# One tile in two halves for the conversion of w_out, a later split of the second unit of factors, half as many unread products, masks loaded first

## The chip, the cores and the metric

The kernel runs on one core of a Trainium2 chip. The metric is the device time of one execution in microseconds (us). TensorE (PE) multiplies, VectorE (DVE) and ScalarE (ACT) work element by element, SyncE (SP) issues all DMAs of this kernel, and GpSimd (POOL) only fills a few constants. Each engine takes its instructions strictly in the order in which they were written for it; an instruction that waits for a semaphore holds up everything behind it on its engine.

## The reference

Inputs are float32 in the reference; the weights reach the chip as 64-bit patterns (float64), so the kernel has to turn them into float32 itself.

```python
# attention: 4 batches, 8 heads, 576 positions, 64 dims; heads 0-3 see a local window of 32,
# heads 4-7 see the positions at a stride of 32
scores = (q @ k.T) / 8 ; scores = where(mask, scores, -1e9)
attn   = softmax(scores) ; attn_out = attn @ v            # 2304 tokens x 512
# first gated block
a = x @ w1 ; b = x @ w2 ; h = (a * b) @ w3 ; x = h @ w_out # 512 -> 1024 -> 1024 -> 512
# second block
h = x @ w_in                                               # 512 -> 2048
g = h * (1 / (1 + exp(-1.702 * h)))
out = g @ w_out                                            # 2048 -> 512
```

## The kernel before

Every float32 matrix is held as a high and a low part in a rounded format; a product of two matrices is three matmuls (high by low, low by high, high by high). `split_hi` (L171, ACT) makes the high part, `split_lo` (L177, DVE) the low part.

A weight unit arrives as raw 64-bit words (1024 KB) and goes through `to_f32`: two ACT instructions (L192 writes the float32 tile, L193 rewrites half of the raw words in place), then three on DVE (L194, L195, L196).

Stage 1 is the attention of batch 0. ACT and DVE do the softmax and the first weight units; PE has little to do, and `busy` (L496 to L498) puts matmuls between whose result, in the tile `spare`, nothing reads: two for each of 44 places.

Then PE carries the rest: the first block of batches 0 to 3 (L354 makes the products with w1 and w2, L400 the product with the joined w3 and w_out, `ysb` L406 copies it out and `ydram` keeps it), with the attention of the next batch woven in. While batch 3 runs, the eight units of the second block's w_out (called here w_out units 1 to 8; 8 to 15 in the code) are converted by `u_conv` (L541): load the raw words (L538, tile `raw`, two of them, one in pool `cv_a`, one in `cv_b`), `to_f32` into the tile `x` (pool `cv_a`, one buffer), load the raw words of the unit after next, write `x` to DRAM (`wodram`, 512 KB, L555). The tile `x` has 2048 columns, of which w_out uses the first 1024.

The second block works on 768 tokens at a time with seven products per unit in place of eight (`quad`, L679 and on; eight units per 768 tokens). Its factors of w_in come from DRAM (`widram`) in `w_load` (L613), into the same tile `x`, and are split into `hl`. The units of w_out come back from `wodram` in `wt_load` (L641) through the `raw` tile of `cv_a`, and are split into `w`. A `quad` makes seven products of six matmuls each (L666); ACT copies the first one out of PSUM into a tile `c` (L684), DVE adds the others (L672), gelu (L657, L658), and `o_group` (L712) multiplies the gelu of the unit before by w_out, nine matmuls each, one group in the middle of the quad (`mid`) and one behind it. PSUM tiles `ps` come from the pool `mm` with four buffers: a fifth product waits until a copy has freed one.

The pool `p2`, from which `c` and the other small tiles of the second block come, is opened where the first block's pools and `cv_b` were closed, so its tiles lie where `ysb` and the `raw` tile of `cv_b` lay.

The order on each engine is made by a scheduler from the order of the program: `weave` sorts pieces of work by a place between 0 and 1, and the scheduler then moves an instruction ahead of others where its own estimate says that it is ready earlier. So edits at one place can change the order at another.

Of the kernel before, what the change touches and what calls it, by code (L numbers as in the profile page):

```python
# [11 lines left out]
F32 = mybir.dt.float32  # L12
F32R = mybir.dt.float32r
# [8 lines left out]
P = 128  # L22
# [22 lines left out]
CW2 = 1024  # L45
# [3 lines left out]
NB = NT // BT  # L49
NU = 8  # L50
# [87 lines left out]
def body(ctx: ExitStack, tc, qk, vv, mask, w1, w2, w3t, wo, win, wout, out):  # L138
    nc = tc.nc
# [29 lines left out]
    def split_hi(hi, src, eng="act"):  # L169
        if eng == "act":  # L170
            nc.scalar.activation(hi, src, AF.Copy)  # L171
        else:
            nc.vector.tensor_copy(hi, src)

    def split_lo(lo, src, hi, eng="dve"):
        e = nc.vector if eng == "dve" else nc.gpsimd
        e.tensor_tensor(lo, src, r(hi), op=ALU.subtract)  # L177
# [46 lines left out]
    def a_load(n):  # L224
        if n >= n_all or n in raws:
            return
        tl = ALL[n]
        nk, w = tl.nk, 2 * (tl.nq + tl.nk)
        t = at.tile([P, ATW], F32, tag="qk", name="qk", bufs=3)
        nc.sync.dma_start(t[:, :w], qk[n, :, :w])  # L230
        u = at.tile([P, HL * D], F32, tag="v", name="v", bufs=4)
        nc.sync.dma_start(u[:nk], vv[n, :nk])
        raws[n] = (t, u)
# [249 lines left out]

    nc.gpsimd.memset(band[0], 0.0)
    nc.gpsimd.memset(band[1], 0.0)
    a_load(0)
    nc.sync.dma_start(msk, mask)
    a_load(1)
    for i in range(2):
        c_load(i)  # L490
# [3 lines left out]
    nc.vector.tensor_copy(identb, ident)  # L494

    def busy():  # L496
        for _ in range(2):
            nc.tensor.matmul(spare, identb, msk.rearrange("p m n -> p (m n)"), start=True, stop=True)  # L498

    weave(steps_for(0), list(zip((0.1, 0.5), conv(0, 1))), [busy] * 44)  # L500
# [29 lines left out]
    cv = None  # L530
# [9 lines left out]

    def u_conv(i, last=False):  # L541
        raw = todo.pop(i)
        x = cv[0].tile([P, 2 * CW2], F32, tag="x", name="x")
        to_f32(x[:, :CW2], raw, CW2)
        if not last:
            u_load(i + 2)
        if i < NU:
            a21, a11, a12, a22, s1, s2, s3, s4 = (x[:, n * 256:(n + 1) * 256] for n in range(8))
            nc.vector.tensor_tensor(s1, a21, a22, op=ALU.add)
            nc.vector.tensor_tensor(s2, s1, a11, op=ALU.subtract)  # L550
            nc.vector.tensor_tensor(s3, a11, a21, op=ALU.subtract)
            nc.vector.tensor_tensor(s4, a12, s2, op=ALU.subtract)
            nc.sync.dma_start(widram[i], x[:, 256:])
        else:
            nc.sync.dma_start(wodram[i - NU], x[:, :CW2])  # L555

    def u_convs(lo, hi, ahead=True):
        return [lambda i=i: u_conv(i, not ahead and i + 2 >= hi) for i in range(lo, hi)]
# [51 lines left out]

    wq = {}

    def w_load(n):  # L613
        if n < NB * NU:
            t = (p2 if n % 2 else cv_a).tile([P, 2, 7 * 256], F32R, tag="hl", name="hl")
            x = cv_a.tile([P, 2 * CW2], F32, tag="x", name="x")[:, 256:]
            nc.sync.dma_start(x, widram[n % NU])
            split_hi(t[:, 0], x)
            split_lo(t[:, 1], x, t[:, 0])
            wq[n] = t  # L620

    g = batch_groups(3)
    weave(
        g, [(0.02 + 0.06 * kk, lambda kk=kk: y_prep(0, kk)) for kk in range(2)] + [(0.09, lambda: w_load(0))]
        + [(0.1, lambda: u_load(NU)), (0.11, lambda: u_load(NU + 1))]
        + [(0.14 + 0.7 * i / NU, f) for i, f in enumerate(u_convs(NU, 2 * NU))],
    )
    p1s.close()
    right2.close()
# [8 lines left out]
    gl, gr = {}, {}  # L638
    acc_l, acc_r = {}, {}

    def wt_load(i):  # L641
        t = cv_a.tile([P, CW2], I64, tag="raw", name="raw").bitcast(F32)[:, :CW2]
        nc.sync.dma_start(t, wodram[i])
        w = wt[i].rearrange("p a c n -> p a (c n)")
        split_hi(w[:, 0], t)
        split_lo(w[:, 1], t, w[:, 0])

    def g_split(src):
        t = ring[used[0] % len(ring)]
# [58 lines left out]
    def o_group(acc, g, i, half):  # L708

        for t in range(HT // P):  # L710
            for a, c in ORDER:
                nc.tensor.matmul(  # L712
                    acc[t], g[:, a, t * P:(t + 1) * P], wt[i][:, c, half],
                    start=(i == half == 0 and (a, c) == ORDER[0]),
                    stop=(i == NU - 1 and half == 1 and (a, c) == ORDER[-1]),
                )
# [8 lines left out]
                nc.scalar.activation(ob, acc[t], AF.Copy)  # L725
            nc.sync.dma_start(out[c0 + t * P:c0 + (t + 1) * P, :], ob)

    wt_load(0)
    w_load(1)
    for b in range(NB):  # L730
        left = [accp.tile([P, 512], F32, tag="acc", name="acc") for _ in range(HT // P)]
        for i in range(NU):
            if b == 0 and i + 1 < NU:
                wt_load(i + 1)
            quad(b, i, (lambda i=i: o_group(left, gl.pop(i - 1), i - 1, 0)) if i else (lambda: None))
            if i:
                o_group(left, gl.pop(NU + i - 1), i - 1, 1)
        for h in range(2):
            o_group(left, gl.pop(h * NU + NU - 1), NU - 1, h)
        put(left, b * BT)  # L740
        if b + 1 < NB:
            for kk in range(2):
                y_prep(b + 1, kk)
        right = [mm.tile([P, 512], F32, tag="mm", name="acc") for _ in range(HT // P)]
        for i in range(NU):
            for h in range(2):
                o_group(right, g_split(gr.pop(h * NU + i)), i, h)
        put(right, b * BT + HT)
# [35 lines left out]
```

## Time and profile before

| | us |
|---|---|
| median of 3 runs (lowest, highest) | 878.0 (876.34, 879.31) |
| the profiled execution's own time | 878.23 |
| its span, first to last instruction | 876.4 |
| PE busy in the span | 833.2 (95%) |
| DVE busy | 587.2 (67%) |
| ACT busy | 437.9 (50%) |
| mean granted clock of PE, 1 is 2.4 GHz | 0.982 |

Busy time is the union of an engine's instructions. Matmuls overlap one another, so the sum of their durations is more than the time they take. Times inside the trace count from the first instruction.

### The profile page before, as it was taken

How to read it: one execution, taken by the hardware profiler on the slowest of the kernel's cores; microseconds unless marked ns; L12 is line 12 of the kernel's file. 1: busy time of each engine (PE TensorE's matmuls, PEld its weight loads, DVE VectorE, ACT ScalarE, POOL GpSimd, SP SyncE). 2: the span in 40 equal slices, each digit the busy share in tenths (PEclk: the TensorE clock that was granted, in tenths of full speed). 3: DMA queues.
4: the chain of work that ended last, by engine and by line, in shares of the span. 5: the costliest groups of instructions: out<-in, count | busy, mean ns of one | idle time of the engine just before them, and what ended most of it. 6: DMA issues, size and time to landing. Idle time of an engine off the chain costs nothing.

```text
span 876.4 us, 14097 instructions
## 1 busy us (share of the span) xinstructions
PE 833.2 (95%) x5288; PEld 744.0 (85%) x5288; DVE 587.2 (67%) x1369; ACT 437.9 (50%) x996; POOL 1.4 (0%) x8
## 2 busy tenths in 40 slices
PE   6999999999999999999993399999999999999998
PEld 3589899987889999999993389988999988999986
DVE  5999882368767778656342688876487765677740
ACT  6998762257565464444332455554244543434430
POOL 0000000000000000000000000000000000000000
PEclk9999999999999999999997699999999999999999
DMA  7765551244577553133445445213222232222010
GB/s 258 245 218 174 167 188 58 68 145 156 200 248 231 190 189 117 56 141 127 138 148 164 162 141 188 86 43 109 82 95 73 81 106 87 79 84 85 1 37 36
DMA packets 41700, 114.03 MB, mean 130 GB/s; under 512 B 4512, under 2 KB 25888, under 8 KB 38048
## 3 DMA queue, kind: packets, MB, share of 16 engines
q1 hardware_dynamic: 41632, 113.13, 37.9%
q8 instruction: 41, 0.67, 0.3%
q14 instruction: 27, 0.22, 0.1%
HBM read 88.60 MB, written 24.51 MB: 129 GB/s over the span
## 4 chain that ended last, share of the span: by engine, by line
PE 75%; DMA 9%; DVE 7%; ACT 7%; issue 1%; SPq 0%; ACTq 0%; DVEq 0%
PE acc L712 22%; PE ps L666 19%; PE ps L354 18%; PE ps L400 8%; DMA wodram<-x 4%; PE acc L469 2%; PE sc L250 2%; PE pv L308 2%; ACT sm L260 2%; DMA raw<-in_wout 1%; DMA x<-widram 1%; PE spare L498 1%; DVE x L196 1%; DVE x L195 1%; PE pt L286 1%
## 5 line engine op out<-in xcount | busy, mean ns | idle before, releaser
L666 PE MATMUL ps<-yq,hl 128*128 128x384 f32 x1008 | 188.9, 342 | 27.6 <-ACT c L684 21.7
L666 PEld LDWEIGHTS ps<-yq,hl 128*128 128x128 f32 x1008 | 181.3, 191 | 32.9 <-ACT c L684 22.2
L712 PE MATMUL acc<-w,w 128*128 128x512 f32 x864 | 205.2, 391 | 1.2 <-ACT w L171 1.2
L712 PEld LDWEIGHTS acc<-w,w 128*128 128x128 f32 x864 | 161.3, 188 | 34.4 <-ACT w L171 2.2
L400 PE MATMUL ps<-ab,w 128*128 128x288 f32 x768 | 108.1, 298 | 1.3 <-DVE ab L177 1.3
L400 PEld LDWEIGHTS ps<-ab,w 128*128 128x128 f32 x768 | 102.5, 188 | 4.6 <-DVE ab L177 2.4
L354 PE MATMUL ps<-xbh,w 128*128 128x288 f32 x512 | 103.4, 295 | 0.0
L354 PE MATMUL ps<-xah,w 128*128 128x288 f32 x512 | 102.1, 295 | 0.0
L354 PEld LDWEIGHTS ps<-xbh,w 128*128 128x128 f32 x512 | 82.2, 188 | 0.1
L354 PEld LDWEIGHTS ps<-xah,w 128*128 128x128 f32 x512 | 81.9, 188 | 0.0
L354 PE MATMUL ps<-xbl,w 128*128 128x288 f32 x256 | 79.6, 311 | 0.0
L354 PE MATMUL ps<-xal,w 128*128 128x288 f32 x256 | 76.4, 299 | 0.9 <-ACT abf L377 0.8
L657 ACT ACTIVATE sg<-c 128x384 f32<-128x384 f32 x48 | 25.1, 525 | 103.7 <-DVE c L672 103.5
L260 ACT ACTIVATE sm<-sm,st 96x128 f32<-96x128 f32 (+2 forms) x176 | 67.7, 388 | 17.7 <-DVE st L255 17.6
L193 ACT ACTIVATE raw<-raw 128x1024 int32<-128x1024 uint32 (+1 forms) x44 | 42.7, 972 | 48.3 <-DMA raw<-in_wout 32.2
L672 DVE TENSOR_TENSOR u<-ps,u 128x384 f32<-128x384 f32 x96 | 53.2, 554 | 11.2 <-PE ps L666 9.1
L177 DVE TENSOR_TENSOR hl<-x,hl 128x1792 fp32r<-128x1792 f32 x24 | 48.6, 2024 | 16.4 <-ACT hl L171 16.4
L379 DVE TENSOR_TENSOR abf<-ps,abf 128x288 f32<-128x288 f32 x64 | 28.9, 451 | 37.8 <-PE ps L354 31.6
L354 PEld LDWEIGHTS ps<-xbl,w 128*128 128x128 f32 x256 | 48.0, 188 | 3.8 <-issue 0.3
L171 ACT ACTIVATE ab<-abf 128x288 fp32r<-128x288 f32 x64 | 27.6, 442 | 46.4 <-DVE abf L379 39.0
L255 DVE CUSTOM_DVE_ANT_0 sm<-sc,msk 96x128 f32<-96x128 f32 (+2 forms) x176 | 40.9, 276 | 13.9 <-PE sc L250 8.4
L354 PEld LDWEIGHTS ps<-xal,w 128*128 128x128 f32 x256 | 48.0, 187 | 2.3 <-ACT abf L377 1.0
(82 smaller groups left out, 1061.2 us busy)
## 6 DMA issues: line engine op xcount, KB each, us to landing
x<-widram SPq DMA_DIRECT2D x24, 896.0 KB
raw<-in_w3t SPq DMA_DIRECT2D x17, 512.0 KB
raw<-in_w SPq DMA_DIRECT2D x8, 1024.0 KB
raw<-in_win SPq DMA_DIRECT2D x8, 1024.0 KB
raw<-in_wout SPq DMA_DIRECT2D x8, 1024.0 KB
widram<-x SPq DMA_DIRECT2D x8, 896.0 KB
qk<-in_qk SPq DMA_DIRECT2D x24, 224.0 KB
ydram<-ysb SPq DMA_DIRECT2D x32, 144.0 KB
```

Source lines behind the costliest of these rows:

```text
L171: nc.scalar.activation(hi, src, AF.Copy)
L177: e.tensor_tensor(lo, src, r(hi), op=ALU.subtract)
L193: nc.scalar.activation(ri[:, :, 0], ru[:, :, 0], AF.Copy, scale=LOW)
L255: nc.vector.tensor_tensor_reduce(sm[:nq, h, :nk], sc[:nq, h // 2, h % 2 * P:h % 2 * P + nk], msk[:nq, mi, :nk], -SCALE, 3e38, op0=ALU.add, ...
L260: nc.scalar.activation(sm[:nq, h, :nk], sm[:nq, h, :nk], AF.Exp, bias=st[:nq, 0, h:h + 1], scale=-1.0, accum_out=st[:nq, 1, h:h + 1],)
L354: nc.tensor.matmul(ps, ws[a][m // 2][:, at:at + P], xh[c][:, k, cols], start=(k == 0 and (a, c) == ORDER[0]), stop=(k == KC - 1 and (a, c) ...
L379: nc.vector.tensor_tensor(f, ps, f, op=ALU.mult)
L400: nc.tensor.matmul(st[0], wfs[a][k][:, n * P:(n + 1) * P], hold[hb, k][:, c], start=(k == 0 and (a, c) == ORDER[0]), stop=(k == MC - 1 and ...
L657: nc.scalar.activation(sg, src, AF.Sigmoid, scale=1.702)
L666: nc.tensor.matmul(ps, w[:, a, f * 256 + kk * P:f * 256 + (kk + 1) * P], yq[:, b, kk, c], start=(kk == 0 and (a, c) == ORDER[0]), stop=(kk ...
L672: nc.vector.tensor_tensor(dst, x, y, op=ALU.add)
L712: nc.tensor.matmul(acc[t], g[:, a, t * P:(t + 1) * P], wt[i][:, c, half], start=(i == half == 0 and (a, c) == ORDER[0]), stop=(i == NU - 1 ...
```

## The change

Six edits:

- The masks' DMA is issued ahead of the first attention tile's.
- `busy` issues one unread matmul at each of its 44 places in place of two.
- The eight w_out units share one tile `x` for all of the stage. Odd and even units take its two halves of 1024 columns, by turns.
- The places of the w_out conversions in `weave` go from 0.14 + 0.7 i/8 to 0.12 + 0.6 i/8.
- `w_load` and `wt_load` are parted into a fetch (the DMA) and a split (ACT and DVE).
- Ahead of the first `quad`, only the fetches of factor unit 1 and w_out unit 1 are written; their splits, and the whole load of w_out unit 2, are written at `mid` of the first quad, behind the copy of its first product. The other w_out units follow one quad each, as before.

```diff
@@ -483,8 +483,8 @@
 
     nc.gpsimd.memset(band[0], 0.0)
     nc.gpsimd.memset(band[1], 0.0)
+    nc.sync.dma_start(msk, mask)
     a_load(0)
-    nc.sync.dma_start(msk, mask)
     a_load(1)
     for i in range(2):
         c_load(i)
@@ -494,7 +494,7 @@
     nc.vector.tensor_copy(identb, ident)
 
     def busy():
-        for _ in range(2):
+        for _ in range(1):
             nc.tensor.matmul(spare, identb, msk.rearrange("p m n -> p (m n)"), start=True, stop=True)
 
     weave(steps_for(0), list(zip((0.1, 0.5), conv(0, 1))), [busy] * 44)
@@ -540,7 +540,12 @@
 
     def u_conv(i, last=False):
         raw = todo.pop(i)
-        x = cv[0].tile([P, 2 * CW2], F32, tag="x", name="x")
+        if i < NU:
+            x = cv[0].tile([P, 2 * CW2], F32, tag="x", name="x")
+        else:
+            if i == NU:
+                todo["x"] = cv[0].tile([P, 2 * CW2], F32, tag="x", name="x")
+            x = todo["x"][:, i % 2 * CW2:(i % 2 + 1) * CW2]
         to_f32(x[:, :CW2], raw, CW2)
         if not last:
             u_load(i + 2)
@@ -610,20 +615,29 @@
 
     wq = {}
 
-    def w_load(n):
+    def w_fetch(n):
         if n < NB * NU:
-            t = (p2 if n % 2 else cv_a).tile([P, 2, 7 * 256], F32R, tag="hl", name="hl")
             x = cv_a.tile([P, 2 * CW2], F32, tag="x", name="x")[:, 256:]
             nc.sync.dma_start(x, widram[n % NU])
+            wq[n] = x
+
+    def w_split(n):
+        if n < NB * NU:
+            x = wq[n]
+            t = (p2 if n % 2 else cv_a).tile([P, 2, 7 * 256], F32R, tag="hl", name="hl")
             split_hi(t[:, 0], x)
             split_lo(t[:, 1], x, t[:, 0])
             wq[n] = t
+
+    def w_load(n):
+        w_fetch(n)
+        w_split(n)
 
     g = batch_groups(3)
     weave(
         g, [(0.02 + 0.06 * kk, lambda kk=kk: y_prep(0, kk)) for kk in range(2)] + [(0.09, lambda: w_load(0))]
         + [(0.1, lambda: u_load(NU)), (0.11, lambda: u_load(NU + 1))]
-        + [(0.14 + 0.7 * i / NU, f) for i, f in enumerate(u_convs(NU, 2 * NU))],
+        + [(0.12 + 0.6 * i / NU, f) for i, f in enumerate(u_convs(NU, 2 * NU))],
     )
     p1s.close()
     right2.close()
@@ -638,12 +652,18 @@
     gl, gr = {}, {}
     acc_l, acc_r = {}, {}
 
-    def wt_load(i):
+    def wt_fetch(i):
         t = cv_a.tile([P, CW2], I64, tag="raw", name="raw").bitcast(F32)[:, :CW2]
         nc.sync.dma_start(t, wodram[i])
+        return t
+
+    def wt_split(i, t):
         w = wt[i].rearrange("p a c n -> p a (c n)")
         split_hi(w[:, 0], t)
         split_lo(w[:, 1], t, w[:, 0])
+
+    def wt_load(i):
+        wt_split(i, wt_fetch(i))
 
     def g_split(src):
         t = ring[used[0] % len(ring)]
@@ -725,14 +745,20 @@
                 nc.scalar.activation(ob, acc[t], AF.Copy)
             nc.sync.dma_start(out[c0 + t * P:c0 + (t + 1) * P, :], ob)
 
-    wt_load(0)
-    w_load(1)
+    w_fetch(1)
+    first_wt = wt_fetch(0)
+
+    def mid_first():
+        w_split(1)
+        wt_split(0, first_wt)
+        wt_load(1)
+
     for b in range(NB):
         left = [accp.tile([P, 512], F32, tag="acc", name="acc") for _ in range(HT // P)]
         for i in range(NU):
-            if b == 0 and i + 1 < NU:
+            if b == 0 and 0 < i < NU - 1:
                 wt_load(i + 1)
-            quad(b, i, (lambda i=i: o_group(left, gl.pop(i - 1), i - 1, 0)) if i else (lambda: None))
+            quad(b, i, (lambda i=i: o_group(left, gl.pop(i - 1), i - 1, 0)) if i else mid_first if b == 0 else (lambda: None))
             if i:
                 o_group(left, gl.pop(NU + i - 1), i - 1, 1)
         for h in range(2):
```

The scheduler's order, with the waits of each row in brackets (the number behind a name tells tiles apart; DMAHW0 to 7 are the eight DMA semaphores, used by turns).

On ACT, where batch 3 starts and the first w_out units are converted, before (`x` L192 and `raw` L193 are the conversion, `hl` the split of the first factor unit, `ysb`, `abf`, `ab` belong to batch 3):

```order
L171 ACTIVATE hl_4814<-x_4815 128x1792 [waits DMAHW2_49]
L171 ACTIVATE ab_4962<-abf_4715 128x288 [waits DVE_49]
L377 ACTIVATE abf_4716<-ps_4965 128x288 [waits PE_49,Activation_49]
L192 ACTIVATE x_4854<-raw_4819 128x1024 [waits DVE_49]
L171 ACTIVATE ab_4993<-abf_4716 128x288 [waits DVE_49]
L377 ACTIVATE abf_4717<-ps_4996 128x288 [waits PE_49]
L171 ACTIVATE ab_5033<-abf_4717 128x288 [waits DVE_49]
L406 ACTIVATE ysb_5061<-ps_5036 128x288 [waits DMAHW6_49,PE_49]
L193 ACTIVATE raw_4860<-raw_4860 128x1024 [waits DMAHW3_49,Activation_49]
L406 ACTIVATE ysb_5098<-ps_5064 128x288 [waits DMAHW7_49,PE_49]
L192 ACTIVATE x_4925<-raw_4835 128x1024 [waits DMAHW4_49]
L406 ACTIVATE ysb_5126<-ps_5101 128x288 [waits DMAHW5_49,PE_49,Activation_49]
```

The same place on ACT in the changed kernel:

```order
L171 ACTIVATE hl_4772<-x_4770 128x1792 [waits DMAHW2_49]
L171 ACTIVATE ab_4917<-abf_4671 128x288 [waits DVE_49]
L377 ACTIVATE abf_4672<-ps_4928 128x288 [waits PE_49,Activation_49]
L192 ACTIVATE x_4793<-raw_4775 128x1024 [waits DVE_49]
L192 ACTIVATE x_4793<-raw_4791 128x1024
L171 ACTIVATE ab_4956<-abf_4672 128x288 [waits DVE_49]
L377 ACTIVATE abf_4673<-ps_4959 128x288 [waits PE_49]
L171 ACTIVATE ab_4987<-abf_4673 128x288 [waits DVE_49]
L406 ACTIVATE ysb_5023<-ps_4998 128x288 [waits DMAHW6_49,PE_49]
L193 ACTIVATE raw_4799<-raw_4799 128x1024 [waits DMAHW3_49,Activation_49]
L406 ACTIVATE ysb_5051<-ps_5026 128x288 [waits DMAHW7_49,PE_49]
L192 ACTIVATE x_4793<-raw_4799 128x1024 [waits DMAHW4_49]
```

Before, each unit has a tile of its own in one buffer (x_4854, x_4925), and the second L192 waits for DMAHW4, the write of the first. Now both write x_4793, the second L192 stands right behind the first with no wait, and the third is the first that waits for a write.

On ACT, where the first quad begins, before (`w0_66` and `w2_68` are the high parts of w_out units 1 and 2, `c` L684 the copy of the first product):

```order
L193 ACTIVATE raw_5148<-raw_5148 128x1024 [waits DMAHW0_49,DVE_49]
L192 ACTIVATE x_5211<-raw_5083 128x1024 [waits DMAHW1_49]
L406 ACTIVATE ysb_5546<-ps_5521 128x288 [waits DMAHW2_49,PE_49,Activation_49]
L193 ACTIVATE raw_5217<-raw_5217 128x1024 [waits DMAHW5_49,DVE_49,Activation_49]
L192 ACTIVATE x_5282<-raw_5148 128x1024 [waits DMAHW6_49]
L192 ACTIVATE x_5368<-raw_5217 128x1024 [waits DMAHW7_49,DVE_49]
L171 ACTIVATE w0_66<-raw_5555 128x1024 [waits DMAHW0_49]
L684 ACTIVATE c_5578<-ps_5571 128x384 [waits DMAHW3_49,DVE_49,DMAHW4_49,PE_49,Activation_49]
L171 ACTIVATE w2_68<-raw_5567 128x1024 [waits DMAHW1_49]
```

The same place in the changed kernel (`w4_70` is unit 3, `hl` factor unit 1, `c` now L704):

```order
L377 ACTIVATE abf_4681<-ps_5355 128x288 [waits PE_49,Activation_49]
L171 ACTIVATE w0_66<-raw_5506 128x1024 [waits DMAHW4_49]
L171 ACTIVATE ab_5383<-abf_4681 128x288 [waits DVE_49]
L406 ACTIVATE ysb_5411<-ps_5386 128x288 [waits DMAHW3_49,PE_49]
L171 ACTIVATE w2_68<-raw_5553 128x1024 [waits DMAHW6_49]
L406 ACTIVATE ysb_5439<-ps_5414 128x288 [waits PE_49]
L406 ACTIVATE ysb_5467<-ps_5442 128x288 [waits DMAHW7_49,PE_49,Activation_49]
L171 ACTIVATE w4_70<-raw_5605 128x1024 [waits DMAHW2_49]
L406 ACTIVATE ysb_5495<-ps_5470 128x288 [waits DMAHW1_49,PE_49,Activation_49]
L704 ACTIVATE c_5518<-ps_5511 128x384 [waits DMAHW3_49,DVE_49,DMAHW4_49,PE_49,Activation_49]
L171 ACTIVATE hl_5548<-x_5504 128x1792 [waits DMAHW0_49]
```

Before, the copy `c` stands behind three conversions and one split of w_out; now all conversions are further ahead, three splits of w_out stand among the four copies `ysb` of batch 3, and `hl` has moved from behind the first quad's gelus to right behind `c`.

On SP, at the end of the conversions, before (`wodram<-x` writes a converted unit, `raw<-wodram` fetches it back, `x<-widram` fetches factors):

```order
L555 DMA wodram_87<-x_5211 128x1024 [waits DMAHW6_49]
L555 DMA wodram_87<-x_5282 128x1024 [waits DMAHW7_49,DVE_49]
L643 DMA raw_5555<-wodram_87 128x1024 [waits DMAHW0_49,Activation_49]
L643 DMA raw_5567<-wodram_87 128x1024 [waits DMAHW1_49,DMAHW0_49,DVE_49]
L555 DMA wodram_87<-x_5368 128x1024 [waits DMAHW2_49,DVE_49]
L617 DMA x_5560<-widram_86 128x1792 [waits DMAHW6_49,DMAHW7_49,DMAHW3_49,DMAHW2_49]
L643 DMA raw_5656<-wodram_87 128x1024 [waits DMAHW4_49,DMAHW1_49,DVE_49]
```

The same place in the changed kernel:

```order
L560 DMA wodram_87<-x_4793 128x1024 [waits DMAHW3_49,DVE_49]
L657 DMA raw_5506<-wodram_87 128x1024 [waits DMAHW7_49,Activation_49]
L560 DMA wodram_87<-x_4793 128x1024 [waits DMAHW5_49,DVE_49]
L657 DMA raw_5553<-wodram_87 128x1024 [waits DMAHW6_49,DMAHW4_49,DVE_49]
L408 DMA ydram_84<-ysb_5411 128x288 [waits Activation_49]
L621 DMA x_5504<-widram_86 128x1792 [waits DMAHW5_49,DMAHW3_49,DMAHW0_49]
L408 DMA ydram_84<-ysb_5439 128x288 [waits DMAHW1_49,Activation_49]
L657 DMA raw_5605<-wodram_87 128x1024 [waits DMAHW6_49,DMAHW2_49,DVE_49]
L408 DMA ydram_84<-ysb_5467 128x288 [waits Activation_49]
L408 DMA ydram_84<-ysb_5495 128x288 [waits Activation_49]
```

The fetches of w_out units 1 to 3 and of factor unit 1 now stand among the last copies of batch 3 to `ydram`, where before all of these copies were ahead of them.

## Rows read from the trace of the kernel before

**Rows 1.** Windows (us: PE, PEld, DVE, ACT, POOL busy, clock, DMA share, GB/s).

```profile
460.00:472.00 12.00, 7.65 (x48) 7.33 (x47) 2.94 (x4) 2.97 (x4) 0.00 (x0) 0.97 0.54 169
472.00:482.00 10.00, 0.56 (x2) 0.05 (x1) 1.61 (x3) 2.22 (x2) 0.00 (x0) 0.50 0.49 157
482.00:494.00 12.00, 0.00 (x0) 0.00 (x0) 7.25 (x7) 2.50 (x3) 0.00 (x0) 0.50 0.30 100
```

**Rows 2.** Timeline of PE, 440 to 530 (start, us, work, idle before).

```profile
450.34 12.85 PE L400 MATMUL ps<-ab,w 128*128 128x288 f32 x96
...
463.03 3.29 PE L666 MATMUL ps<-yq,hl 128*128 128x384 f32 x18
470.67 1.89 PE L666 MATMUL ps<-yq,hl 128*128 128x384 f32 x6 [4.35 <-ACT ysb L406]
494.23 5.33 PE L666 MATMUL ps<-yq,hl 128*128 128x384 f32 x18 [21.66 <-ACT c L684]
```

**Rows 3.** Chain that ended last, in order of time (start, us, work).

```profile
520.85 2.08 PE acc L712 x9
...
528.16 4.24 PE ps L666 x24
532.40 2.08 PE acc L712 x9
```

**Rows 4.** The same chain, during the conversions.

```profile
407.20 1.15 ACT x L192
...
410.60 1.24 DVE x L196
...
411.90 6.46 DMA raw<-in_wout
...
450.17 6.80 DMA wodram<-x
...
456.99 1.13 ACT x L192
...
461.77 7.41 DMA wodram<-x
```

**Rows 5.** Groups by line, 404 to 494 (busy, mean ns, idle before).

```profile
L192 ACT ACTIVATE x<-raw 128x1024 f32<-128x1024 f32 x8 | 9.0, 1123 | 7.9 <-DMA wodram<-x 7.2 <-DVE hl L177 0.5
L193 ACT ACTIVATE raw<-raw 128x1024 int32<-128x1024 uint32 x6 | 6.8, 1127 | 32.0 <-DMA raw<-in_wout 32.0
```

**Rows 6.** The chain again, from the last conversion on.

```profile
493.55 3.86 DMA wodram<-x
...
497.43 4.79 DMA x<-widram
...
502.24 1.71 ACT hl L171
...
503.98 2.04 DVE hl L177
```

**Rows 7.** Timeline of ACT, 488 to 495.

```profile
489.56 1.06 ACT L171 ACTIVATE w<-raw 128x1024 fp32r<-128x1024 f32 x1 [0.30 <-DMA raw<-wodram]
493.68 0.49 ACT L684 ACTIVATE c<-ps 128x384 f32<-128x384 f32 x1 [3.06 <-DVE x L196]
```

**Rows 8.** Windows of stage 1, columns as in the first group.

```profile
0.00:22.00 22.00, 15.05 (x90) 8.16 (x91) 12.93 (x49) 14.59 (x38) 1.42 (x8) 1.00 0.74 259
22.00:49.00 27.00, 26.66 (x218) 14.93 (x216) 25.37 (x99) 26.78 (x87) 0.00 (x0) 1.00 0.69 240
```

**Rows 9.** Timelines of PE, ACT and DVE, 0 to 52.

```profile
3.41 1.17 PE L250 MATMUL sc<-qk 64*96 64x128 f32 x8 [3.41 <-DMA qk<-in_qk]
...
9.62 3.62 PE L498 MATMUL spare<-msk,identb 128*128 128x512 bf16 x8
...
13.59 0.49 ACT L288 ACTIVATE ps<-pt 128x384 f32<-128x384 f32 x1 [1.12 <-PE pt L286]
...
4.95 0.29 DVE L255 CUSTOM_DVE_ANT_0 sm<-sc,msk 96x128 f32<-96x128 f32 x1 [4.95 <-DMA msk<-in_mask]
```

## The prediction

> **What bounds the kernel now.** I read the windows first. For most of the span PE is busy; the large hole lies between the two blocks. From 472 to 494 PE works 0.56 us of 22 at a granted clock of 0.50, the lower of its two levels, while DVE and ACT are busy 8.9 and 4.7 us [rows 1]. No engine bounds this stretch.
>
> PE's timeline says what is waited for. The last group of batch 3 ends at 450.34 + 12.85 = 463.2. Eighteen matmuls of the first quad follow, then 4.35 us of waiting for a copy `ysb`, six more matmuls, and 21.66 us of waiting for the copy `c` of the first product [rows 2]. ACT's timeline shows that `c` is ready to go in all but one thing: it waits until a conversion's last instruction on DVE is done [rows 7], since it lies where a raw tile of the conversions lay. So the first quad waits for the last w_out unit.
>
> The chain shows what the conversions wait for. It goes from write to write: 450.17, 461.77 [rows 4]. One unit costs 11.6 us: 6.8 us of the write of the unit before, then 4.8 us for L192, the three DVE instructions and the issue. The single tile `x` makes it serial. ACT waits 32.0 us for loads before L193, which can run ahead, and then still 7.2 us for the write before L192, which can't [rows 5].
>
> What the hole costs, counted to the third quad's first output group at 520.85 [rows 3]: from 463.2 that is 57.7 us. The work in it is seven products, a whole quad and four products. A whole quad takes 532.40 - 520.85 = 11.55 us; without its two groups of 2.08 it takes 7.4; four products take 4.24 [rows 3]. That is 23.2 us, so **34.5 us are lost**: 26.0 in the two waits, 2.0 for eighteen matmuls at the lower clock (5.33 against 3.29 [rows 2]), some 6.5 in later waits for the next factors, whose fetch stands behind the last conversion (4.79 us of fetch, 1.71 and 2.04 of split, and the same again [rows 6]). This is the most the edits around the hole can give.
>
> **The two halves.** L192 of unit 1 starts at 407.20 and its last DVE instruction ends at 411.8 [rows 4]. In the new order L192 of unit 2 stands right behind it and waits for nothing, so unit 2 is done some 3 us later, at 415.1; unit 1, which shares DVE with it, at 412.2. From then on each half turns by itself: load and write go out together, the write comes back, and 4.8 us of ACT, DVE and issue follow, plus 0.5 for which I let the two halves and batch 3's copies be in each other's way. The other leg, a load of 6.46 [rows 4] and L193 of 1.13 [rows 5], is 7.6, about as long as the write.
>
> How long a write takes with two halves in flight the trace doesn't show. At the low end it is the 6.8 of now: the engines move 157 GB/s at a share of 0.49 [rows 1], so there is room for twice as much, just. At the high end every transfer waits for the other half's, twice 7.41 = 14.8 us. I take 8.0, near the low end, because the halves start at different times and part of a transfer is latency that others can use. A turn of two units is then 8.0 + 4.8 + 0.5 = 13.3 us (12.1 to 20.1). Unit 8 is done at 415.1 + 3 * 13.3, and 2 us more since its L192 is behind copies of batch 3: **457**, against 493.5 now.
>
> **What is late next.** ACT takes its work in order, and the new order puts conversions that wait for loads between the copies of batch 3's products. At this pace I work through the last products: the four PSUM tiles run out for about 2 us. Then the last `ab` stands behind unit 8 and the split `w0_66`, at 457 + 2.4 = 459.4. PE's last block needs it after 21 of 96 matmuls; the other 75 at 12.85/96 end at 469.4, so **batch 3 ends 6.2 us later** than the 463.2 of now.
>
> The copy `c` now stands behind three splits of w_out and the last `ysb`. Unit 2's fetch goes out when `w0_66` is done on DVE (459) and takes 3.9, as a write of the same size does [rows 6]; split 1.06 on ACT [rows 7] and some 1.2 on DVE: 465.2. Unit 3 the same way: ACT is through with it at 470.3. The last `ysb` follows at 470.7, its way to DRAM takes some 2 us more (some quarter of a w_out unit's bytes, which take 3.86), and `c` goes at 473. PE begins the first quad at 469.4, needs the last `ysb` at 472.7 and `c` at 473.7: no wait worth naming. The quad ends at 476.8. The next factors, fetched at about 462, are split behind `c`: 473.5 + 1.71 on ACT, then four additions and 2.04 on DVE make 477.8, 1.0 us late. The third quad's first group comes at 477.8 + 11.55 + 4.24 = 493.6, which is 27.2 us before 520.85. I take off 0.5 for a possible fall of the clock during a 4 us wait (in the trace the clock in 460 to 472 averages 0.97 with PE idle from 466.3 for 4.35 us, so such a wait is just about enough [rows 1, 2]) and 1.0 for what I have not seen: **25.7 us**. Everything behind is as before.
>
> The later split of factor unit 1 and of w_out unit 1 has its price in these sums; the new places of the conversions in the weave order them and cost nothing by themselves.
>
> **Masks first, half of the unread products.** The first reduction on DVE starts at 4.95, when the masks land; the first scores start at 3.41, when their tile lands [rows 9]. With the masks first the scores start about 0.5 later, at 3.9, and the reduction can't start before they are done, 4.5 to 5.1. That is a gain of 0.4 or a loss of 0.2; I take 0.
>
> In 22 to 49 ACT is busy 26.78 of 27 us and DVE 25.37; PE's 26.66 are largely unread products [rows 8]. So ACT's work bounds this stage, and what the products cost is delay ahead of a transpose or a score that ACT waits for. The one such wait I can point to is 1.12 us before the copy at 13.59, behind eight unread matmuls of 3.62 us in which two transposes had to wait [rows 9]; four stand there now. I take a gain of **1.0 us**, between 0 and 2.5 (ACT's idle time between 5 and 22 is not much more), and a loss is the rival on the clock.
>
> The sum is made against the profiled execution's 878.2 (span 876.4 and 1.8 around it), which is the median of 878.0 within the spread: 878.2 - 25.7 - 1.0 = **851.5**.
>
> **The rivals.** *Transfers keep their time.* With writes of 6.8 and less delay on ACT, unit 8 is done at about 453. The last `ab` comes early enough that batch 3 ends at 464 to 465, and the chain of w_out fetches decides: `c` at about 469.5, third quad's group at 489.4, 31 us gained, 846. For it: the share of 0.49. Against it: the overlap of load and write that already makes a write 6.8 to 7.4 long, where one beside a smaller load takes 3.86 [rows 4, 6]. Chance 0.18. The Trainium skill (DMA: Bandwidth & Descriptors, "Anatomy of one DMA") gives about 2 us fixed and the rest at 436 GB/s; for a load and a write together, 1.57 MB, that would be an estimated 5.6 us, and this rival or better. The trace's 6.8 to 7.4 doesn't agree with it.
>
> *Contention.* Writes of 10.7 make a turn of 16 us and put unit 8 at 465. All that follows is 8 us later, and PE's waits get long enough for the lower clock, 2 us: 17 gained, 860 to 861. Chance 0.15.
>
> *The clock in stage 1.* With fewer unread products PE has gaps late in the stage, the clock falls, and the scores, transposes and products of the attention take twice their time. Some 15 us of real matmuls lie in 22 to 49, and ACT would wait for a part of them: 6 us, 858. For it: the clock fell after an idle PE in 460 to 472 [rows 1]. Against it: in 0 to 22 PE is busy only 15.05 of 22, with the clock at 1.00 [rows 8]. Chance 0.07. The Trainium skill (TensorE: Matmul & The Clock Gate, "HAM oscillation") warns of just this: the gate takes the clock back where the engine idles, and short work between waits pays for it each time; by it alone the halving would be a loss.
>
> *The change doesn't do what it says*: the halves wait for each other after all, since they are one tile. Then the cycle stays 11.6 per unit and the time within 1 us of 878. The rows of the order speak against it: no wait between the first two. Chance 0.02.
>
> *Slower: ACT's queue.* Loads that take much longer hold the copies of batch 3 up so far that PE loses more there than the hole gives back. It decides from where unit 8 is done 27 us later than I say, at 484: turns of 22.5 us, writes of 17, more than twice the longest in the rows. Each further us of a turn costs three. At 24 us it would be 882. Chance 0.03.
>
> **The numbers.** Forecast 851.5 with 0.55; its own range 848 to 856. The range for 8 in 10 reaches to the fast rival and to contention and the clock: 843 to 864. What a measurement tells from no change is about 0.3%, 2.6 us. Faster 0.94, same 0.02, slower 0.04.
>
> **What would show it.** L192 of the second w_out unit right behind the first; eight conversions done at 450 to 462 in place of 493.5; writes of 7 to 9 us; PE's wait for `c` gone or under 3 us; new waits of PE for `ab` before the last block of batch 3, 2 to 6 us; the third quad's first group 22 to 31 us earlier; the first block starting 0 to 2.5 earlier, with the clock at 1.00 in stage 1. I am wrong if the writes take over 11 us, if `c` still waits for a conversion, or if PE's waits inside batch 3 exceed 10 us.

## The result and the profile after

The changed kernel takes **849.9 us** (median of 4 runs, 848.5 to 850.65), the kernel before 877.2 on the same chip. The ratio of the two is 0.9686, with a 95% interval of 0.966 to 0.9712: faster by 2.9 to 3.4%. The forecast was 851.5, range 843 to 864.

The profiled execution took 850.65 us with a span of 848.9, against 878.23 and 876.4 before. PE is busy 97% of the span. The windows of after, to be read beside those of before [rows 1, 8] (us of PE, weight load, DVE, ACT, POOL, then the granted clock, DMA share, GB/s):

```profile
22.00:49.00 27.00, 21.33 (x178) 14.52 (x175) 24.76 (x106) 26.06 (x86) 0.00 (x0) 0.83 0.66 224
...
458.00:494.00 36.00, 34.73 (x200) 33.70 (x201) 24.10 (x36) 19.23 (x28) 0.00 (x0) 0.95 0.51 178
```

The hole is gone: PE works 34.73 of the 36 us from 458 to 494. But in stage 1 the clock, 1.00 before [rows 8], has fallen to a mean of 0.83. One term of the forecast paid off. Beside it the lower clock of one of the rivals has come; what it costs is a question for the experiments.

The chain that ended last, in order of time (start, us, work), answers to that of the conversions before [rows 4]:

```profile
408.35 1.16 ACT x L192
...
416.30 8.04 DMA wodram<-x
424.36 1.18 ACT x L192
...
429.18 9.27 DMA wodram<-x
438.47 0.95 ACT x L192
...
443.42 7.97 DMA raw<-in_wout
...
459.27 10.92 PE ps L400 x69
```

Before, each unit's L192 waited for the write of the unit just before. Now the links from L192 to L192 span two units: 408.35, 424.36, 438.47, and then a load paces it (the next L192 of this half starts at 452.72). A write got longer (8.04 and 9.27 against 6.80 and 7.41), but two are under way at a time.

PE's timeline answers to [rows 2]:

```profile
452.87 3.84 PE L400 MATMUL ps<-ab,w 128*128 128x288 f32 x27 [0.95 <-ACT abf L377]
459.27 10.92 PE L400 MATMUL ps<-ab,w 128*128 128x288 f32 x69 [2.57 <-DVE ab L177]
470.02 11.73 PE L686 MATMUL ps<-yq,hl 128*128 128x384 f32 x66
...
493.07 2.25 PE L732 MATMUL acc<-w,w 128*128 128x512 f32 x9
```

The wait of 21.66 us for `c` is gone, and so is that of 4.35 for `ysb`. New is the 2.57 us for the last `ab`, behind unit 8. The third quad's first group comes at 493.07 in place of 520.85 [rows 3]. ACT's timeline shows why `c` no longer matters; before, it went at 493.68 behind a conversion [rows 7]:

```profile
472.57 0.49 ACT L704 ACTIVATE c<-ps 128x384 f32<-128x384 f32 x1 [1.89 <-DMA ydram<-ysb]
472.96 1.70 ACT L171 ACTIVATE hl<-x 128x1792 fp32r<-128x1792 f32 x1
```

### The profile page after: what moved, and what is told of

Same layout as the page of the kernel before. It is cut to its first block, busy times and chain, and to the rows that moved or that the text cites. A ratio compares the mean times of both kernels' runs of the same rounds, so it can differ in the third digit from the quotient of the medians.

```text
span 848.9 us, 14010 instructions
## 1 busy us (share of the span) xinstructions
PE 824.6 (97%) x5244; PEld 741.9 (87%) x5244; DVE 586.3 (69%) x1369; ACT 436.7 (51%) x996; POOL 1.4 (0%) x8
## 4 chain that ended last, share of the span: by engine, by line
PE 82%; DMA 6%; ACT 6%; DVE 5%; issue 1%; SPq 0%; ACTq 0%; DVEq 0%
PE acc L732 23%; PE ps L354 21%; PE ps L686 21%; PE ps L400 8%; PE acc L469 2%; PE sc L250 2%; PE pv L308 2%; DMA wodram<-x 2%; ACT sm L260 2%; PE pt L286 1%; DMA raw<-in_wout 1%; DMA raw<-in_w3t 1%; DMA abf<-abdram 1%; DVE x L195 1%; DMA ydram<-ysb 1%
## 5 line engine op out<-in xcount | busy, mean ns | idle before, releaser
L686 PE MATMUL ps<-yq,hl 128*128 128x384 f32 x1008 | 183.7, 337 | 0.0
L686 PEld LDWEIGHTS ps<-yq,hl 128*128 128x128 f32 x1008 | 177.7, 188 | 3.6
L400 PE MATMUL ps<-ab,w 128*128 128x288 f32 x768 | 110.3, 301 | 6.3 <-DVE ab L177 5.2
L193 ACT ACTIVATE raw<-raw 128x1024 int32<-128x1024 uint32 (+1 forms) x44 | 43.0, 976 | 27.7 <-DMA raw<-in_wout 11.4
L379 DVE TENSOR_TENSOR abf<-ps,abf 128x288 f32<-128x288 f32 x64 | 28.9, 452 | 34.6 <-PE ps L354 29.3
```

The source lines that it names most:

```text
L193: nc.scalar.activation(ri[:, :, 0], ru[:, :, 0], AF.Copy, scale=LOW)
L379: nc.vector.tensor_tensor(f, ps, f, op=ALU.mult)
L400: nc.tensor.matmul(st[0], wfs[a][k][:, n * P:(n + 1) * P], hold[hb, k][:, c], start=(k == 0 and (a, c) == ORDER[0]), stop=(k == MC - 1 and ...
L686: nc.tensor.matmul(ps, w[:, a, f * 256 + kk * P:f * 256 + (kk + 1) * P], yq[:, b, kk, c], start=(kk == 0 and (a, c) == ORDER[0]), stop=(kk ...
```

## The experiments

Each ran beside the kernel before on the same chip; times are medians, and the ratio to before carries the 95% interval. Where two variants differ by 2 or 3 us, I compare their ratios. A hundredth of a ratio is 8.8 us, and the interval of a difference of two ratios is about 0.003 either way (2.6 us).

**Halves alone.** The kernel before, with this edit only:

```diff
-        x = cv[0].tile([P, 2 * CW2], F32, tag="x", name="x")
+        if i < NU:
+            x = cv[0].tile([P, 2 * CW2], F32, tag="x", name="x")
+        else:
+            if i == NU:
+                todo["x"] = cv[0].tile([P, 2 * CW2], F32, tag="x", name="x")
+            x = todo["x"][:, i % 2 * CW2:(i % 2 + 1) * CW2]
```

> Kernel before with one edit, the two halves of one tile x for the eight w_out units; splits, unread products and masks as before. Theory A (the halves double the pace of the serial chain of write and conversion, and that is the whole gain): 850 to 854 us, w_out unit 8 done near 456 in place of 493.5, and at most 3 us lost against the whole change because the copy c stands behind more splits. Rival B (the later split of the factors carries a part of its own): 857 to 866 us, PE waits several us for c or for the second factors although unit 8 is done at 456. Rival C (halves bring nothing alone): 875 to 878.

853.15 us, ratio 0.9709 (0.9689 to 0.9729): 25.6 us of gain from one edit. That is theory A's figure, and B and C are out. PE's waits for the last `ab` and then for `c` are small:

```profile
459.59 9.40 PE L400 MATMUL ps<-ab,w 128*128 128x288 f32 x69 [2.75 <-DVE ab L177]
...
474.95 1.96 PE L671 MATMUL ps<-yq,hl 128*128 128x384 f32 x6 [1.80 <-ACT c L689]
```

**All but the halves.** The kernel after, with a tile `x` per unit, as before.

> Kernel after without the halves: each w_out unit takes a tile x of its own from the pool's one buffer, as before; later split, one unread product and masks first are kept. Theory A: the cycle of 11.6 us per unit is back and unit 8 is done near 493, so 873 to 880 us. Rival B (the later split carries a part): 862 to 872 us, with the waits for factors behind c shorter though unit 8 is as late as before.

877.43 us, 0.9983 (0.9965 to 1.0001). The hole is back as it was; from PE's timeline:

```profile
492.76 5.24 PE L681 MATMUL ps<-yq,hl 128*128 128x384 f32 x18 [21.22 <-ACT c L699]
```

Put in or taken out, the halves are worth some 26 us, and all else together between nothing and 3.

**The late split undone.** The fetches and splits ahead of the first quad stand again as before; the diff is cut, the lines of `mid_first` and its call, which go too, are left out.

```diff
-    w_fetch(1)
-    first_wt = wt_fetch(0)
...
+    wt_load(0)
+    w_load(1)
```

> Kernel after with the second factors' and first w_out unit's split ahead of the first quad again. On ACT the split hl then stands ahead of the copy c, 1.7 us. Theory A (the split's place is worth little once unit 8 is early): 849.5 to 852.5 us. Rival B: 855 to 862 us, since c waits for a factor split that itself waits for the last ysb's way to DRAM, and PE's four PSUM tiles run out.

850.79 us, 0.9683 (0.9662 to 0.9704), as after. On ACT the split of the next factors now stands ahead of `c`, and PE waits 2.2 us for `c`. It doesn't show in the total.

**Two unread products again**, and, for measure, **after once more** on the chip of the runs that follow.

```diff
-        for _ in range(1):
+        for _ in range(2):
```

> Kernel after with two unread products at each of the 44 places again. Theory A1 (the gain of stage 1 is taken back by waits for w3 between 177 and 230, so stage 1 doesn't count): 849 to 851 us, same within 0.2%. Theory A2 (as forecast, halving carried 1.0 us): 850.5 to 852. Rival clock (the lower clock of 0.83 in 22 to 49 with one product costs real time in PE and on ACT): clock 1.00 again in 22 to 49 and 844 to 848 us.

> The kernel after, unchanged, beside the next kernels on the same chip, as their measure. 849 to 851.5 us if the stage-1 difference seen with two unread products (848.6) is real; 848 to 849.5 if that was the scatter of executions.

Two products: 848.63 us, 0.9658 (0.9639 to 0.9678). After again: 849.79, 0.9681 (0.9661 to 0.9701). So two are no worse than one, and better by 2.0 us if the middle of the intervals is believed; the forecast had them worse. The time lies between the ranges of the first theory and of the rival, in neither. The windows of the kernel with two products show the clock back:

```profile
22.00:49.00 27.00, 26.28 (x218) 15.17 (x216) 25.60 (x103) 26.12 (x83) 0.00 (x0) 1.00 0.71 237
```

What ACT waited for between 12 and 60 us bounds what the clock can cost there (us in total, times, longest). First after:

```profile
ACT xbh L171 <- PE pv L308: 3.4, 3, 1.3
ACT abf L377 <- PE ps L354: 1.0, 2, 0.6
...
ACT ps L288 <- PE pt L286: 0.2, 1, 0.2
```

Then with two products:

```profile
ACT ps L288 <- PE pt L286: 1.3, 2, 0.9
...
ACT xbh L171 <- PE pv L308: 0.3, 1, 0.3
ACT abf L377 <- PE ps L354: 0.2, 1, 0.2
```

ACT bounds this stage in both. With one product it waits 3.9 us more for attention products and first-block products (the first two rows of after); 1.1 of it come back, since it waits less for transposes. All its waits together are 5.4 us in after and 2.9 with two products, a difference near the 2.0 of the times. But not all of it stands where the clock is low. The first of the three waits in the first row of after comes at a clock of 1.00, behind ten unread products that PE had to do before the attention product:

```profile
14.69 0.33 ACT L171 ACTIVATE xbh<-pv 128x192 fp32r<-128x192 f32 x1 [1.34 <-PE pv L308]
```

From 40 to 60 us alone ACT waits 3.9 us with one product and 1.1 with two.

**No loads beside the writes.** w_out units 3 to 8 convert again the raw words of units 1 and 2.

```diff
-        if not last:
+        if i >= NU: todo[i + 2] = raw
+        elif not last:
             u_load(i + 2)
```

> Kernel after without the loads of w_out units 3 to 8: these convert again the raw words of units 1 and 2 (so most of w_out's values are left out). Theory (a write is 8 to 9 us because the load issued with it shares the DMA engines): writes of 4 to 5 us, near the 3.86 of a write beside a small load; a turn of two units about 4.5 + 4.8 = 9.3 in place of 13.3, unit 8 done at 444 to 448 in place of 457, batch 3 ends 5 us earlier, c with it: 842 to 846 us. Rival (a write's length is its own, whatever else is in flight): writes of 7 to 9, unit 8 at 455 to 458, 848 to 851.

845.63 us, 0.962 (0.9605 to 0.9636), some 5 us below after. SP issues the first two writes, and ACT's fourth L192 waits for the second of them:

```profile
414.50 2.96 SPq L562 DMA_DIRECT2D wodram<-x  x2
```

```profile
419.80 1.16 ACT L192 ACTIVATE x<-raw 128x1024 f32<-128x1024 f32 x1 [0.16 <-DMA wodram<-x]
...
428.62 1.14 ACT L192 ACTIVATE x<-raw 128x1024 f32<-128x1024 f32 x1
...
438.28 1.15 ACT L192 ACTIVATE x<-raw 128x1024 f32<-128x1024 f32 x1
```

The second write, issued at 414.50 + 2.96 − 0.32 (one issue) = 417.1, lands at 419.8: 2.7 us where one beside loads takes 8.0 to 9.3; I had expected 4 to 5. A turn of the half of these two rows and the row between them is 8.8 and 9.7 us where it was 14.1 and 14.3 (13.6 and 12.1 in the other half). The run takes away the loads, and with them most of the overlap of the two halves' writes; so the length of a write comes from what is in flight beside it, and the rival "own length" is out. PE's timeline shows where this gain ends:

```profile
464.80 4.33 PE L688 MATMUL ps<-yq,hl 128*128 128x384 f32 x24
469.46 3.58 PE L688 MATMUL ps<-yq,hl 128*128 128x384 f32 x19 [0.33 <-ACT c L706]
473.78 4.33 PE L688 MATMUL ps<-yq,hl 128*128 128x384 f32 x23 [0.73 <-DVE hl L177]
```

Batch 3 is no longer held up (it ends at 464.8), and from there the chain goes from fetch to fetch of w_out's first units (455.56, 461.80, 468.07, of 3.87, 3.90 and 3.19 us), with `c` between them.

**Units 7 and 8 converted in the second block**, in the quad that splits them, without the way through DRAM; then the same with two unread products.

```diff
     def wt_load(i):
-        wt_split(i, wt_fetch(i))
+        if i < NU - 2:
+            wt_split(i, wt_fetch(i))
+            return
+        raw = cv_a.tile([P, CW2], I64, tag="raw", name="raw")
+        nc.sync.dma_start(raw, wout[i])
...
+        to_f32(t, raw, CW2)
```

The diff is cut: left out are the two split lines, and the edits by which batch 3 no longer loads and converts these two units.

> Kernel after, but w_out units 7 and 8 are not converted during batch 3: each is loaded raw and converted in the second block, in the quad where it is split, without the way through DRAM. Theory (what is left in the hole is the last ab standing behind units 7 and 8, and the clock after it): unit 6 is done near 445, the last ab no longer late, batch 3 ends 5 to 7 us earlier, at 463 to 465, and the copy c decides, at about 467 to 470: 844 to 847 us. The added work is 2 x 5.5 us of DVE and ACT in quads 6 and 7, where DVE is busy 9.1 of 11: up to 3 us back. Rival (PE has no slack to gain, or DVE in the quads takes it back): 849 to 853.

> The same with two unread products per place, as a kernel that might beat both. If two unread products are worth 0 to 2 us and the direct conversion 4 to 6: 842 to 847 us. If stage 1 is swallowed between 177 and 230: within 0.5 us of the run with one unread product.

850.85 us, 0.968 (0.9661 to 0.9699): no gain, my theory of this run is wrong. Batch 3 is indeed held up less (PE waits 0.22 and 0.67 us for `ab` in its last block, and it ends at 466), but the time goes into a new wait. The chain of the run:

```profile
440.64 4.24 DMA raw<-wodram
444.91 1.07 ACT w L171
...
447.25 3.71 DMA raw<-wodram
...
459.30 4.37 DMA raw<-wodram
...
466.41 3.78 DMA ydram<-ysb
...
473.02 0.50 ACT c L713
```

Four fetches of w_out, one behind the other through one `raw` tile, and then the last `ysb` stand ahead of `c`, which goes at 473.02, against 472.57 in after; counted from the first L192 of w_out that is 0.8 us earlier. With two unread products it takes 847.66, 0.9648 (0.9635 to 0.9662). That is **the lowest of the runs that compute all of the result**, by a ratio lower than after's by 0.0033 (uncertain by 0.0024), though above the 842 to 847 hoped for, and what it adds to two unread products alone is 0.0010, no difference. The second pair of runs again puts two products below one, by 0.0032.

**Stage 1 apart.** The kernel after with both stage-1 edits undone, and with only the masks' place undone:

```diff
-    nc.sync.dma_start(msk, mask)
     a_load(0)
+    nc.sync.dma_start(msk, mask)
```

> Kernel after with both edits of stage 1 undone: two unread products per place and the masks behind the first attention tile; halves and late split kept. Against halves alone (853.15) it shows the late split's worth, against after (849.8) the worth of both stage-1 edits. Forecast's own split (stage 1 worth 1.0): 850.5 to 851. If masks first are worth 2 to 3 us and halving costs about as much: 850 to 852. If the late split is worth 2 us or more: 849 to 851; if nothing: 852.5 to 854.

> Kernel after with only the masks behind the first attention tile again, one unread product per place. If the masks' place is worth 0 (forecast): 849.5 to 851. If masks first are worth 2 to 3 us: 852 to 853.

851.42 us, 0.9687 (0.967 to 0.9703), and 852.12, 0.9714 (0.9688 to 0.974). With the two runs above they make a square:

| ratio to before | two unread | one unread |
|---|---|---|
| masks behind | 0.9687 | 0.9714 |
| masks first | 0.9658 | 0.9681 |

Masks first gain 0.0029 and 0.0033, 2.7 us; one product for two costs 0.0023 and 0.0027, 2.2 us. The mean of two differences is uncertain by 0.0021, 1.8 us, so each stands clear of zero, just. The halving has a third pair, that of the direct conversions, with 0.0032. The weak corner is 0.9714: three of its five times are 851.3 to 852.1 us, two are 856.6 and 857.0, and by the medians it would be 0.9698; masks first would then gain 0.0017 in its column, and the halving cost 0.0011 in its row. Together the two edits are worth 0.0006, half a us.

For the masks the timelines agree. PE starts the join of w3 and w_out at 177.28, 178.36 and 178.70 us in the three profiles with two products and the masks behind (before, this run, halves alone), and at 174.28 and 175.84 in the two with two products and the masks first. Part of how their place helps can be read on ACT. The first copy of transposed scores, with two products and the masks behind:

```profile
14.38 0.49 ACT L288 ACTIVATE ps<-pt 128x384 f32<-128x384 f32 x1 [2.34 <-PE pt L286]
```

and with the masks first:

```profile
13.35 0.49 ACT L288 ACTIVATE ps<-pt 128x384 f32<-128x384 f32 x1 [0.43 <-PE pt L286]
```

With the masks behind, eight unread products stand between the first two transposes and the last two. With the masks first, all four transposes stand together behind them. In before, with the same order as in the first of these rows, the copy goes at 13.59 [rows 9], so the order on PE accounts for 0.2 to 1.0 us here; the rest I can't point to.

Beside halves alone (0.9709), the first of these two runs differs by the late split: 0.0022 less, uncertain by 0.0026. In the pair further above the late split was worth nothing. Between 0 and 2 us; it stays open.

**None and three.** One unread product in all of stage 1, and three at each place.

> Kernel after with one unread product in all of stage 1 in place of 44. Theory clock (unread products keep PE's clock at 2.4 GHz and their lack costs time): clock well under 0.83 in 22 to 49, ACT waits for PE, 852 to 860 us. Theory delay (each unread product stands in front of a transpose or a score): the stage gets shorter, 847 to 849. Theory neither (ACT bounds the stage, and what moves is the order): 849 to 852.

> Kernel after with three unread products per place. Theory clock: clock 1.00, no better than two products (847.5 to 849.5). Theory delay: each further product costs, PE is over 27 of 27 us busy in 22 to 49, 852 to 860.

854.74 us, 0.9727 (0.9712 to 0.9742), and 864.09, 0.9833 (0.9815 to 0.985), above both ranges I had given for it. With 2, 1 and next to none the time is 848.6, 849.8 and 854.7, and with 3 it is 864.1. Without them the windows of PE (busy, clock, DMA share, GB/s) show the clock falling from about 42 us on:

```profile
34.00:40.00 6.00, 4.51 (x41) 1.00 0.39 110
40.00:44.00 4.00, 2.51 (x26) 0.80 0.72 216
44.00:48.00 4.00, 3.57 (x28) 0.50 0.75 259
48.00:52.00 4.00, 3.67 (x25) 0.50 0.42 109
52.00:56.00 4.00, 4.00 (x21) 0.50 0.10 32
```

The theory of the clock has its time, but not the number I gave (0.88 in 22 to 49, not well under 0.83): the low clock comes later and lasts longer. The order of the engines changed here too. With three the clock is 1.00, and the first product of the first block starts at 57.6 us against 48.1 with two. The whole loss lies in stage 1, but the order of all engines changed with the third product, so I can't say how much of it is delay and how much order.

## Why the prediction was right, step by step

**The hole.** −25.7 was forecast. The third quad's first group came 27.8 us earlier by the timelines (493.07 against 520.85), and the halves by themselves are worth 26 in two pairs of runs. Counted from the first L192 of w_out, which removes what lies upstream, the gain is 520.85 − 407.20 = 113.65 against 493.07 − 408.35 = 84.72: 28.9, and 30.0 in the profile of after once more. I had taken off 1.5 for a fall of the clock and for the unseen; without it I had 27.2. The links, forecast and measured: write with two halves in flight 8.0, 8.0 to 9.3; unit 8 done 457, its write issued at 457.4; last `ab` 459.4, PE goes on at 459.27; batch 3 ends 469.4, at 470.0 to 470.2; `c` at 473, at 472.57; third quad's group 493.6 before the take-offs, 493.07.

Such an agreement link by link is in part luck. In the link to the end of batch 3 two misses cancel: 69 matmuls were left behind the last `ab`, not 75, and they took 10.92 us, not the 9.2 of 69 in 96 of the last block before, since the clock was at its lower level for part of them. The windows of after:

```profile
459.00:461.00 2.00, 1.73 (x8) 1.73 (x9) 0.22 (x1) 0.41 (x1) 0.00 (x0) 0.66 0.79 252
461.00:463.00 2.00, 2.00 (x11) 2.00 (x10) 0.00 (x0) 0.53 (x1) 0.00 (x0) 0.50 0.86 298
```

In after once more, behind a wait of the same 2.57 us, the clock was 1.00 from 458 to 494 and the same 69 took 9.38 us. Of the eight profiles in which 69 are left, three show the 10.92 and five 9.38 to 9.40, so the 0.5 taken off for such a fall was a fair price.

The rival *transfers keep their time* lost by the 8.0 to 9.3. The run without loads shows its path: batch 3 ended at 464.8 (464 to 465 forecast for it), `c` and the chain of fetches decided, and the third quad's group came at 489.42 (489.4). That the two times fit so well is luck, since its writes are shorter than the rival's 6.8 and its first L192 came 2.4 us later than in before. The Trainium skill (DMA: Bandwidth & Descriptors, "Anatomy of one DMA") has a fit for single DMAs that GpSimd issues; for a write of 512 KB it would give an estimated 3.2 us. The 2.7 us without loads, issued by SyncE, are near that; the fit has no term for what else is in flight, and there the 8.0 to 9.3 decide.

**Stage 1, −1.0: wrong in both parts, and nearly right in the sum by luck.** I held that the masks' place is worth 0 and that halving the unread products gains 1.0. Measured: masks first gain some 2.7, halving costs some 2.2.

For the masks, the step that failed is the landing at 4.95 [rows 9], taken from one profile. The first reduction waits for the masks until 5.39, 5.47 and 5.65 us in the three others with the masks behind; with the masks first it starts at 4.90 to 5.16. That is worth up to 0.7 us. The new order of the transposes on PE, which I had not seen, is worth 0.2 to 1.0 at the first copy, this delay included; where the rest of the 2.7 comes from stays open.

For the products, the step that failed is "what the products cost is delay ahead of a transpose or a score". The wait of 1.12 us [rows 9] was there, but an order with the transposes together nearly removes it, whatever their number (0.43 with two products, none with one or three). What the halving would do to the clock I left to a rival with a chance of 0.07. "Half" is not what the scheduler made of it either. The lines of the unread products, first after, then with two (ns shortest, median, longest, then first and last start):

```profile
L498 PE MATMUL spare<-msk,identb x44: 377/379/634, 8.9 to 27.2; 128*128 128x512 bf16 x44
...
L498 PE MATMUL spare<-msk,identb x88: 377/379/634, 9.4 to 46.4; 128*128 128x512 bf16 x88
```

With one product a place the last starts at 27.2 us, and none is left for the rest of the stage. In 22 to 49 they had been 58, 15.24 us and some half of PE's 26.66, not "largely" all of it; now they are 15. So the rival's condition came true: the clock was 0.50 from 40 to 52 us. Its price was not 6 us. The halving's whole cost is some 2, and that it is the clock's is not shown: PE starts the join of w3 and w_out at 175.80 and 175.76 us in the two profiles of after and at 175.84 with two products, level, though the other pair (direct conversion) is 3.5 us apart there. What differs in every pair lies behind the join, at a clock of 1.00 (see below). The Trainium skill (TensorE: Matmul & The Clock Gate, "HAM oscillation") had warned of the fall of the clock, and here the trace agrees: between short pieces of work with waits, PE ran at the lower clock.

I had argued from the first 22 us, in which PE is busy 15.05 and keeps a clock of 1.00 [rows 8], that late gaps would not matter. That was the wrong place to look: in the same kernel after, the first 22 us (15.41 busy) are at 1.00 as well, and the clock falls from 40 on. The windows of after:

```profile
34.00:40.00 6.00, 3.63 (x45) 0.98 0.64 227
40.00:44.00 4.00, 2.65 (x20) 0.50 0.45 152
44.00:48.00 4.00, 3.62 (x27) 0.50 0.41 103
48.00:52.00 4.00, 4.00 (x21) 0.50 0.87 336
52.00:56.00 4.00, 4.00 (x30) 0.82 0.33 90
```

**"Everything behind stage 1 as before": not quite.** After is 1.5 us ahead of before where the join of w3 and w_out starts (175.80 against 177.28), and level where the last products of batch 0 start (229.12 and 229.14). Every kernel with one unread product takes 53.1 to 53.4 us from the one to the other, those with two 51.9 to 52.4, though the order of PE and ACT there is the same. With three it is 53.3 as well, and there the clock in stage 1 was 1.00. So about 1 of the 2.2 us that the halving costs arises here, and not in the stretch at the lower clock. ACT's rows show one place: one load of w3, in after again

```profile
201.35 0.65 ACT L193 ACTIVATE raw<-raw 128x512 int32<-128x512 uint32 x1 [1.63 <-DMA raw<-in_w3t]
```

and with two products

```profile
200.56 0.67 ACT L193 ACTIVATE raw<-raw 128x512 int32<-128x512 uint32 x1 [0.77 <-DMA raw<-in_w3t]
```

Why the load comes later stays open, and with it how much of the 2.2 us is the clock's. The new places of the conversions in the weave, which I priced at nothing, change nothing at all: with the old ones the scheduler makes the same order on every engine.

## What to carry to other kernels

A serial chain of write and refill through one buffer shows in the chain of waits as the same transfer over and over; a second buffer, here the unused half of a tile, is worth what a model of the next limits says, if it follows them one after the other (last `ab`, fetches of w_out, `c`) and takes a write's price with the load that will run beside it. When two small edits are forecast by their sum, run each alone: here they were some +2.2 and −2.7 us and looked like nothing. Work that nobody reads may hold PE's clock for the work that somebody waits for; before thinning it out, look where the scheduler puts what is left, and at the clock in the stretch where PE will idle, not at one where it idled before. And a lower clock is not yet a loss: look whether the delay is still there at the next place where all kernels do the same work.

## What the runs showed of the hardware

- A write of 512 KB from SBUF to DRAM landed 2.7 us after its issue with no load in flight (run without loads), in 6.8 and 7.4 beside one load of 1 MB [rows 4], and in 8.0 and 9.3 with the other half's write and load in flight as well (after).
- In after, PE's clock was at its lower level (0.50) from 48 to 52 us while PE was busy 4.00 of 4 us, after 40 to 44 with 2.65 of 4; in the 22 us from the start it was at 1.00 with 15.41 busy.
- The first L192 of w_out started between 406.3 and 409.6 us in four profiles with the same order of stage 1 to batch 2 (after, after again, late split undone, no loads): executions of one order differ by some 3 us upstream, so the hole is better measured from its own first instruction than from the start of the span.
